# Attention with fp32 scores and transposes on row halves of the array, and the decay added by DVE

## The chip, the cores and the metric

The kernel runs on one core of one Trainium2 chip. Times are device microseconds. TensorE is PE, VectorE DVE, ScalarE ACT, GpSimd POOL; SP issues the DMAs. PEld is PE's loading of the stationary operand.

## The reference, cut to what matters

Three stages follow each other: causal attention with a decay, a dense mixture of eight experts, and a feed-forward stage. Only the first is touched. All is fp32.

```
B, H, S, D = 2, 8, 576, 64
scores = q @ k.T / sqrt(D)                  # per batch and head
cum    = cumsum(log(clip(f, 1e-4, 1)))      # per batch and head, over S
scores = scores + cum[i] - cum[j], masked to j <= i
attn   = softmax(scores);  x = attn @ v     # x: 1152 x 512
```

The term cum[i] is the same for a whole row, so the softmax doesn't change if it is left out.

## The kernel before

Work goes by query tiles: five per batch, ten in all (tile 0 to 9), of 128 queries (64 in tiles 4 and 5). A tile of queries that ends at position e sees the keys up to e, rounded up to whole blocks of 128: 128, 256, 384, 512 and 576 keys, in each batch. Within a tile the four pairs of heads are the units. A loop (line 588) makes two steps per unit, one for each head, and is a pipeline written out by hand: a step issues the exponential of the step before, the scores of its own head, a piece of filler, and in every second step the product with v of the unit three earlier (attend) and the transposes of the unit two earlier. Each engine runs its instructions in the order in which the loop issues them.

Products of queries and keys are made in fp32r, in which one pass of the array takes an operand of reduced precision. So q and k are split into a high and a low part (split, lines 308 to 319: a cast, and a subtraction on DVE or POOL), both are transposed on PE together (trans, lines 321 to 350, eight transposes of 128 columns per tile for q and eight for k), and the four tiles that two products need are evacuated or copied by DMA: scores (line 361) multiplies [q high; q high] with [k high; k low] (line 374) and [q low; constants] with [k high; rows of cum] (line 375). Two constants of -1 against two rows with cum in parts add the decay within the product. DVE then adds the mask, negates and takes the smallest value in one instruction (line 387); for 576 keys the scores lie in two PSUM tiles of 288 columns and DVE takes two. ACT makes the exponential and its sum (line 397), POOL multiplies with the reciprocal (normalize, line 413), PE transposes the weights p block by block of 128 keys (lines 429 and 440, in plain fp32), evac (line 273) moves them to SBUF on whichever of ACT and DVE a cost table thinks freer, and attend (line 453) multiplies them with v, the two heads of a unit on the two column halves of the array.

PSUM has eight banks: one for x, two for scores (ps_s), three for transposes (ps_t), two for the filler (ps_f). The filler (line 489) is the first expert on chunks 0 and 1 of x, 28 pieces of three products per chunk, one per step; it starts after tile 2 and after tile 6. Its weights are loaded and split during tiles 1 to 4 (wsplit, line 565). Warming products of the identity stand in front and in the first 16 steps (line 356).

All DMAs are issued by SP in program order: q and k of the tile after next (line 557), v, the rows of cum, the copies of halves (line 301), and the first experts' weights into the two tiles of the pool stage (line 54).

Of the kernel before, what the change touches and what calls it, by code (L numbers as in the profile page):

```python
# [83 lines left out]
def attention_moe_kernel(  # L84
# [46 lines left out]
    with ExitStack() as actx:  # L131
        ap1 = actx.enter_context(tc.tile_pool(name="ap1", bufs=1))
        rawp = actx.enter_context(tc.tile_pool(name="rawp", bufs=3))
# [28 lines left out]
        chl = pt0[1][:16, :, :S]  # L162
        zer = ap1.tile([16, 1], F32, name="zer")
        mask = ap1.tile([128, 704], F32, name="mask")


        sums4 = [ap1.tile([128, 3, 4], F32, name=f"sums{i}") for i in range(4)]
        cd = drp.tile([2, 16, S], F32, name="cd")


        KW = 832
        kbase = (256, 0)
        kt = kp.tile([128, H, KW], FR, name="kt")
        kbf = kp.tile([128, H, KW], FR, name="kb")
        kb = kbf[:96]
        qa = [kp.tile([128, 4, 128], FR, name=f"qa{i}") for i in range(3)]
        qb = [kp.tile([96, 4, 128], FR, name=f"qb{i}") for i in range(3)]

        def q_rows(i, engine=None):
            engine = engine or nc.gpsimd  # L180
            engine.memset(f(qb[i][64:96]), 0.0)
            engine.memset(f(qb[i][64:68]), -1.0)

        def k_rows(lo, hi, engine=None):
            (engine or nc.gpsimd).memset(f(kb[64:96, :, lo:hi]), 1.0)
# [17 lines left out]
        k_rows(256, 384, nc.vector)  # L203
        q_rows(0, nc.gpsimd)
        q_rows(1, nc.gpsimd)
        nc.vector.tensor_scalar(out=ft, in0=ft, scalar1=1e-4, scalar2=1.0, op0=ALU.max, op1=ALU.min)
        nc.vector.tensor_copy(out=idr, in_=idn)

        def cumulate(lo, hi, part=None):
            w = hi - lo  # L210
            if part != 1:
                cumulate_a(lo, hi, w)
            if part != 0:
                cumulate_b(lo, hi)

        def cumulate_a(lo, hi, w):
# [6 lines left out]
        def cumulate_b(lo, hi):  # L223
# [76 lines left out]
        def duplicate(o, i):  # L300
            nc.sync.dma_start(out=f(o), in_=f(i))

        def prep(kind, b, i, slots):
# [17 lines left out]
            def trans(g, early=False):  # L321
# [10 lines left out]
                if kind == "q":  # L332
                    a_, b_ = qa[slots[g]], qb[slots[g]]
                    if early and g:
                        cum_q(b, i, g, slots[g])
# [1036 lines left out]
```

## Time and profile before

| | |
|---|---|
| median of 3 runs | 1121.14 us (1119.29 to 1121.34) |
| profiled execution, first to last instruction | 1123.8 us |
| PE busy | 1109.8 us, 99% |
| DVE, ACT, POOL busy | 852.3, 504.3, 76.7 us |
| bytes moved by DMA | 98.93 MB |

The profiled execution has no other time than its span; it is one execution, and stands 2.7 us above the median of the runs. Products on PE are pipelined and their recorded durations overlap, so the distance between starts tells what one costs. An fp32 product (scores and x, not transposes) leaves two records each.

### The profile page before, as it was taken

Reading aid. Unit: us, or ns where it says so; the run is one execution under the profiler, and the core shown is the slowest. Engines: PE = TensorE matmul, PEld = TensorE weight load, DVE = VectorE, ACT = ScalarE, POOL = GpSimd, SP = SyncE. Lnnn points to the kernel's source line nnn. Section 1 sums busy time; section 2 is a strip of 40 time slices with the busy share of each in tenths; the row PEclk is TensorE's granted clock in tenths of the full one; section 3 lists DMA queues with packets and bytes.
Section 4 is the critical chain, followed back from the end, with each engine's and each line's share of the span. In section 5 each row is a group of like instructions: output and inputs, shape, how many; then the busy total and the mean of one; then the engine's idle time right before and its main releaser. Section 6 shows DMA issues by size and latency. Waiting matters only on the chain.

```text
span 1123.8 us, 17611 instructions
## 1 busy us (share of the span) xinstructions
PE 1109.8 (99%) x6608; PEld 981.3 (87%) x6608; DVE 852.3 (76%) x1850; ACT 504.3 (45%) x1128; POOL 76.7 (7%) x126
## 2 busy tenths in 40 slices
PE   8999999999999999999999999999999999999998
PEld 7677778989889898898988989899898988899996
DVE  7865655957786877868678686887868658998886
ACT  6766643245344253442534424243342335555554
POOL 5535420000000000000000000000000000000000
PEclk8899999999999999999999999999999999999999
DMA  5524212021332313323133241223311675000000
GB/s 124 145 65 105 53 39 76 20 75 42 128 110 77 124 50 130 105 75 132 49 113 110 86 140 58 94 96 111 122 67 57 205 253 198 1 29 1 29 1 29
DMA packets 78058, 98.93 MB, mean 88 GB/s; under 512 B 35190, under 2 KB 39046, under 8 KB 77974
## 3 DMA queue, kind: packets, MB, share of 16 engines
q1 hardware_dynamic: 77974, 97.81, 27.2%
q8 instruction: 52, 0.85, 0.3%
q14 instruction: 32, 0.26, 0.1%
HBM read 74.38 MB, written 19.21 MB: 83 GB/s over the span
## 4 chain that ended last, share of the span: by engine, by line
PE 93%; DVE 4%; ACT 1%; issue 1%; POOL 0%; DVEq 0%; ACTq 0%; POOLq 0%
PE pa L725 41%; PE pb L1080 28%; PE ph L695 11%; PE x L453 2%; PE pt L429 2%; PE pa L525 1%; PE sp L374 1%; PE ph L506 1%; PE pt L325 1%; DVE p L387 1%; PE sp L375 1%; PE x L862 0%; DVE r L973 0%; DVE r L967 0%; PE wt L359 0%
## 5 line engine op out<-in xcount | busy, mean ns | idle before, releaser
L725 PE MATMUL pa<-w2h,big 128*128 128x512 f32 x924 | 299.7, 393 | 1.2 <-DVE hid_b L703 1.2
L725 PEld LDWEIGHTS pa<-w2h,big 128*128 128x128 f32 x924 | 173.7, 188 | 39.7 <-DVE hid_b L703 1.5
L725 PE MATMUL pa<-w2l,big 128*128 128x512 f32 x528 | 207.2, 392 | 0.0
L1109 ACT COPY snap<-pb 128x288 f32<-128x288 f32 x168 | 66.4, 395 | 142.2 <-PE pb L1080 141.9
L725 PEld LDWEIGHTS pa<-w2l,big 128*128 128x128 f32 x528 | 99.3, 188 | 20.7
L703 DVE SCALAR_TENSOR_TENSOR big<-c,big 128x288 fp32r<-128x288 f32 x140 | 64.2, 459 | 69.4 <-ACT big L702 65.4
L702 ACT ACTIVATE big<-c 128x288 fp32r<-128x288 f32 x168 | 74.8, 445 | 91.8 <-DVE c L1114 89.0
L845 DVE SCALAR_TENSOR_TENSOR acc<-pa,P,acc 128x512 f32<-128x512 f32 x132 | 92.8, 746 | 27.2 <-PE pa L725 27.1
L1080 PE MATMUL pb<-xh,ss 128*128 128x288 f32 x448 | 103.9, 296 | 0.0
L1080 PE MATMUL pb<-tt,ss 128*128 128x288 f32 x672 | 103.7, 296 | 0.0
L1080 PEld LDWEIGHTS pb<-tt,ss 128*128 128x128 f32 x672 | 93.8, 188 | 1.0 <-ACT snap L1109 0.8
L1114 DVE TENSOR_TENSOR c<-pb,snap 128x288 f32<-128x288 f32 x168 | 75.9, 452 | 22.5 <-PE pb L1080 22.5
L824 ACT CAST db<-da 128x512 fp32r<-128x512 f32 x32 | 19.9, 621 | 147.8 <-DVE da L815 147.8
L1080 PEld LDWEIGHTS pb<-xh,ss 128*128 128x128 f32 x448 | 76.9, 188 | 0.6 <-DVE c L1114 0.3
L1080 PE MATMUL pb<-xl,ss 128*128 128x288 f32 x224 | 66.5, 297 | 0.0
L1080 PE MATMUL pb<-xh,w1l 128*128 128x288 f32 x224 | 66.2, 296 | 0.0
L1080 PE MATMUL pb<-xl,w1h 128*128 128x288 f32 x224 | 66.2, 295 | 0.0
L1080 PE MATMUL pb<-xh,w1h 128*128 128x288 f32 x224 | 66.1, 295 | 0.0
L725 PE MATMUL pa<-w2h,hid_b 128*128 128x512 f32 x150 | 58.6, 391 | 0.0
L397 ACT ACTIVATE p<-p,nmax 128x256 f32<-128x256 f32 (+6 forms) x80 | 48.4, 605 | 11.0 <-DVE nmax L387 8.4
L75 DVE TENSOR_TENSOR w2l<-stg,w2h 128x512 fp32r<-128x512 f32 x60 | 41.2, 690 | 15.9 <-ACT w2h L74 15.9
L413 POOL TENSOR_SCALAR p<-p,rs 128x256 f32<-128x256 f32 (+6 forms) x80 | 46.7, 596 | 66.4 <-DVE rs L409 42.2
(229 smaller groups left out, 2402.3 us busy)
## 6 DMA issues: line engine op xcount, KB each, us to landing
stg<-in_moe_w_dram SPq DMA_DIRECT2D x64, 512.0 KB
raw<-in_moe_w_in_dram SPq DMA_DIRECT2D x16, 512.0 KB
raw<-in_moe_w_out_dram SPq DMA_DIRECT2D x16, 512.0 KB
w_in_h<-db SPq DMA_DIRECT2D x16, 256.0 KB
w_in_l<-da SPq DMA_DIRECT2D x16, 256.0 KB
w_out_h<-db SPq DMA_DIRECT2D x16, 256.0 KB
w_out_l<-da SPq DMA_DIRECT2D x16, 256.0 KB
out_dram<-acc SPq DMA_DIRECT2D x9, 256.0 KB
```

The costliest lines, as they stand in the source:

```text
L75: (lo_engine or nc.vector).tensor_tensor(out=lo, in0=raw, in1=f(hi), op=ALU.subtract)
L397: nc.scalar.activation(out=p[:n, a, :nk], in_=p[:n, a, :nk], func=AF.Exp, bias=prev, scale=-1.0, accum_out=u["ssum"][:n, 0, a:a + 1],)
L413: nc.gpsimd.tensor_scalar(out=p[:n, a, :nk], in0=p[:n, a, :nk], scalar1=r[:n, a:a + 1], scalar2=1.0, op0=ALU.mult, op1=ALU.mult,)
L429: nc.tensor.transpose(out=pt[:, o + j * n:o + (j + 1) * n], in_=p[:n, a, j * 128:(j + 1) * 128], identity=idn[:n, :n],)
L695: nc.tensor.matmul(out=ph, lhsT=w[wn][kk][:, fs], rhs=x[c][:, kk], start=(kk == 0 and n == 0), stop=(kk == KD - 1 and n == 2),)
L702: nc.scalar.activation(out=hh, in_=ph, func=AF.Relu)
L703: nc.vector.scalar_tensor_tensor(out=hl, in0=ph, scalar=0.0, in1=f(hh), op0=ALU.max, op1=ALU.subtract)
L725: nc.tensor.matmul(out=pa, lhsT=a_[:, ts_], rhs=w[wn][ft_], start=(first and n == 0), stop=(last and n == 2),)
L845: nc.vector.scalar_tensor_tensor(out=acc[t], in0=pa, scalar=P[:, t, e:e + 1], in1=acc[t], op0=ALU.mult, op1=ALU.add)
L1080: nc.tensor.matmul(out=by_chunk(out_) if len(v_.shape) == 3 else out_, lhsT=u, rhs=v_, start=first and m == 0, stop=m == 5, skip_group_che ...
L1109: nc.scalar.copy(out=t, in_=bank["x", g])
L1114: nc.vector.tensor_tensor(out=t, in0=bank[of, g], in1=snap[with_, g], op=ALU.add)
```

## The change

q and k are no longer split. A row half of the array is its 64 rows 0 to 63 or 64 to 127. The function turn transposes two heads at a time in fp32: the first 64 queries (or keys) on one row half, the other 64 on the other, each into its own PSUM bank; one evacuation per q and per k follows. The heads of a unit then lie on partitions 0 to 63 and 64 to 127 of qt and kt, and scores multiplies both in one step, each on its row half, in fp32 into its own bank; for 576 keys the columns from the tile's start on go to a tile of ps_t. The transposes of p are cut the same way by query halves.

The decay goes out of the products. The negated cum is written to DRAM and read back by DMA to all 128 partitions: bias for the keys in front of the tile, diag for the tile's own keys, which POOL masks (mask_diag). DVE adds bias to the one part of a head's scores and diag to the other (largest), so each head but those of the first tile of a batch takes two instructions. For tile 0, where the DRAM copy would come late, diag is made by eight products of a selecting matrix (pick8) with cum and a DVE addition (spread).

The loop keeps its two steps per unit. Scores stand in the first; attend stands in every fourth step and takes two units; the filler is issued at the end of a step and no longer between scores and attend. ps_t has two tiles of two banks, ps_f one bank. Four of the filler's hidden tiles in its second chunk lie in tiles of stage, which are free when that chunk is done. The DMA copies of halves, the rows of cum and POOL's memsets for the constants are gone.

```
-        hlp = actx.enter_context(tc.tile_pool(name="hlp", bufs=2))
+        rawp = actx.enter_context(tc.tile_pool(name="rawp", bufs=4))
         kp = actx.enter_context(tc.tile_pool(name="kp", bufs=1))
+        mdp = actx.enter_context(tc.tile_pool(name="mdp", bufs=2))
         vp = actx.enter_context(tc.tile_pool(name="vp", bufs=6))
         pp = actx.enter_context(tc.tile_pool(name="pp", bufs=3))
-        ptp = actx.enter_context(tc.tile_pool(name="ptp", bufs=2))
+        ptp = actx.enter_context(tc.tile_pool(name="ptp", bufs=3))
         ps_x = actx.enter_context(tc.tile_pool(name="ps_x", bufs=1, space=PSUM))
         ps_s = actx.enter_context(tc.tile_pool(name="ps_s", bufs=2, space=PSUM))
-        ps_t = actx.enter_context(tc.tile_pool(name="ps_t", bufs=3, space=PSUM))
-        ps_f = actx.enter_context(tc.tile_pool(name="ps_f", bufs=2, space=PSUM))
+        ps_t = actx.enter_context(tc.tile_pool(name="ps_t", bufs=2, space=PSUM))
+        ps_f = actx.enter_context(tc.tile_pool(name="ps_f", bufs=1, space=PSUM))
...
+        KW = 704
+        kbase = (128, 0)
+        kt = kp.tile([128, 4, KW], F32, name="kt")
+        bias = kp.tile([128, H, KW], F32, name="bias")
+        hs1 = kp.tile([128, 12, 128], FR, name="hs1")
+        qt = [kp.tile([128, 4, 128], F32, name=f"qt{i}") for i in range(3)]
...
+        def negate(lo, hi):
+            nc.scalar.mul(out=neg[:, lo:hi], in_=cum[:, lo:hi], mul=-1.0)
+            nc.sync.dma_start(out=cd[:, lo:hi], in_=neg[:, lo:hi])
+        def load_bias(b, lo, hi):
+            nc.sync.dma_start(
+                out=bias[:, :, kbase[b] + lo:kbase[b] + hi],
+                in_=cd[b * H:(b + 1) * H, lo:hi].partition_broadcast(128),
             )
+        diag = {}
+        def span(b, i):
+            s0, n = QT[b][i]
+            return s0, min(S, -(-(s0 + n) // 128) * 128) - s0
+        def load_diag(ti):
+            b, i = tiles[ti]
+            s0, w = span(b, i)
+            diag[ti] = mdp.tile([128, H, 192], F32, tag="md", name="md")
+            nc.sync.dma_start(
+                out=diag[ti][:, :, :w], in_=cd[b * H:(b + 1) * H, s0:s0 + w].partition_broadcast(128)
+            )
+        def mask_diag(ti):
+            b, i = tiles[ti]
+            s0, w = span(b, i)
+            nc.gpsimd.affine_select(
+                out=diag[ti][:, :, :w], in_=diag[ti][:, :, :w], compare_op=ALU.is_ge, fill=NEG, base=0,
+                pattern=[[0, H], [-1, w]], channel_multiplier=1,
+            )
...
+        def turn(kind, ti, us=slice(0, 4)):
+            b, i = tiles[ti]
             s0, n = QT[b][i] if kind == "q" else KTL[i]
...
+            halves = n // 64
+            for u in range(us.start, us.stop):
+                for z in range(halves):
+                    zs = slice(64 * z, 64 * z + 64)
                     nc.tensor.transpose(
+                        out=pt[:, z, 64 * u:64 * u + 64], in_=raw[zs, 2 * u:2 * u + 2].rearrange("p h d -> p (h d)"),
+                        identity=idn[zs, zs],
                     )
+            cols = (us.stop - us.start) * n
+            src = pt[:, :halves, 64 * us.start:64 * us.stop].rearrange("p z (u t) -> p u z t", t=64)
+            if kind == "q":
+                evac(qt[ti % 3][:, us, :n].rearrange("p u (z t) -> p u z t", t=64), src, cols, 0.125)
+            else:
+                o = kbase[b] + s0
+                evac(kt[:, us, o:o + n].rearrange("p u (z t) -> p u z t", t=64), src, cols)
...
+        def scores(u):
+            b, h, n, nk, s0 = u["b"], u["h"], u["n"], u["nk"], u["s0"]
+            k0, g = kbase[b], u["h"] // 2
+            lhs = [qt[u["ti"] % 3][64 * a:64 * a + 64, g, :n] for a in range(2)]
+            sp = [ps_s.tile([128, 512], F32, tag="s", name="sp") for _ in range(2)]
+            rest = nk - s0 if nk > 512 else 0
+            if rest:
+                far2 = ps_t.tile([128, 2, 512], F32, tag="pt", name="far")
+                far = [far2[:, a] for a in range(2)]
+            def product(o, a, lo, hi):
+                nc.tensor.matmul(
+                    out=o, lhsT=lhs[a], rhs=kt[64 * a:64 * a + 64, g, k0 + lo:k0 + hi], start=True, stop=True
+                )
+            for a in range(2):
+                product(sp[a][:n, :nk - rest], a, 0, nk - rest)
+            if rest:
+                for a in range(2):
+                    product(far[a][:n, :rest], a, s0, nk)
+            u["p"] = pp.tile([128, 2, S], F32, tag="p", name="p")
+            u["ssum"] = sums4[(4 * u["ti"] + h // 2) % 4]
+            u["parts"] = []
+            for a in range(2):
+                parts = [(sp[a][:n, :s0], bias[:n, h + a, k0:k0 + s0], 0, s0)] if s0 else []
+                d = far[a][:n, :rest] if rest else sp[a][:n, s0:nk]
+                parts.append((d, diag[u["ti"]][:n, h + a, :nk - s0], s0, nk))
+                u["parts"].append(parts)
+        def largest(u, a):
+            n, p = u["n"], u["p"]
             prev = 3.0e38
+            spent("dve", 110 + 67 + 1.05 * u["nk"])
+            for s_, t_, lo, hi in u["parts"][a]:
                 am = small.tile([128, 1], F32, tag="nmax", name="nmax")
                 nc.vector.tensor_tensor_reduce(
+                    out=p[:n, a, lo:hi], in0=s_, in1=t_, scale=-1.0, scalar=prev, op0=ALU.add, op1=ALU.min,
+                    accum_out=am[:n],
                 )
                 prev = am[:n]
...
+            nb = (nk + 127) // 128
+            halves = n // 64
+            whole = [(a, j) for a in range(2) for j in range(min(nb, 4))]
+            pt = ps_t.tile([128, 2, 512], F32, tag="pt", name="pt")
+            def block(o, z, a, j):
+                zs, w = slice(64 * z, 64 * z + 64), KTL[j][1]
+                nc.tensor.transpose(out=o[:w], in_=p[zs, a, j * 128:j * 128 + w], identity=idn[zs, zs])
+            for o, (a, j) in enumerate(whole):
+                for z in range(halves):
+                    block(pt[:, z, 64 * o:64 * o + 64], z, a, j)
+            jw = min(nb, 4)
+            src = pt[:, :halves, :128 * jw].rearrange("p z (a m) -> p a z m", a=2)
+            dst = pT[:, :, :jw * n].rearrange("p a (j z t) -> p a z j t", z=halves, t=64)
+            parts = [(dst, src)] if 2 * jw * n <= 512 else [(dst[:, a], src[:, a]) for a in range(2)]
...
+                hs = [tuple(hs1[:, 6 * i + 3 * j:6 * i + 3 * j + 3] for j in range(2)) for i in range(2)]
             for i in range(4):
+                if len(hs) == i:
+                    t = stage.tile([128, 2, 512], FR, tag="stg", name="spare")
+                    hs.append(tuple(t[:, j, :CH].rearrange("p (j t) -> p j t", j=3) for j in range(2)))
...
+        def spread(h0):
+            pb = ps_s.tile([128, 512], F32, tag="s", name="pb")
+            for h in range(4):
+                nc.tensor.matmul(
+                    out=pb[:, 128 * h:128 * h + 128], lhsT=pick8[:, h0 + h], rhs=cum[:, :128],
+                    start=True, stop=True,
+                )
+            nc.vector.tensor_tensor(
+                out=diag[0][:, h0:h0 + 4, :128], in0=pb.rearrange("p (h t) -> p h t", h=4),
+                in1=mask.unsqueeze(1).to_broadcast([128, 4, 128]), op=ALU.add,
+            )
+        def turn_half(g):
+            for kind in "qk":
+                turn(kind, 0, slice(2 * g, 2 * g + 2))
+        diag[0] = mdp.tile([128, H, 192], F32, tag="md", name="md")
+        cumulate(128, S)
         warm(8)
+        turn_half(0)
+        spread(0)
         load_v(0, 0)
+        negate(0, S)
+        load_diag(1)
+        load_bias(0, 0, 128)
+        first = [lambda: spread(4), lambda: turn_half(1)]
...
+        for s in range(2 * nu + 10):
...
+                if not a:
+                    scores(units[pi])
+                largest(units[pi], a)
             if s < 16:
                 warm(1)
+            if not a and pi % 2 == 0 and 4 <= pi < nu + 4:
+                for w in units[pi - 4:pi - 2]:
+                    attend(w)
+                if w["h"] == H - 2:
+                    x_out(w)
...
+                    next_loads(ti + 2)
                 elif (st, a) == (0, 1):
+                    turn("q", ti + 1)
                 elif (st, a) == (1, 1):
+                    turn("k", ti + 1)
                     load_v(nb_, ni)
+                if (st, a) == (0, 1) and ti:
+                    load_diag(ti + 1)
+                    lo = [0, 0, 64, 192, 320][ni] if nb_ else 128 * max(ni - 1, 0)
+                    hi = [0, 64, 192, 320, 448][ni] if nb_ else 128 * ni
+                    if hi > lo:
+                        load_bias(nb_, lo, hi)
+                elif (st, a) == (3, 0):
+                    mask_diag(ti + 1)
+            fill()
```

## Rows read from the trace of the kernel before

**Rows 1.** The head of the page: the span, and busy time of each engine.

```profile
span 1123.8 us, 17611 instructions
PE 1109.8 (99%) x6608; PEld 981.3 (87%) x6608; DVE 852.3 (76%) x1850; ACT 504.3 (45%) x1128; POOL 76.7 (7%) x126
```

**Rows 2.** Busy us by stretch: length, PE, PEld, DVE, ACT, POOL, granted clock, DMA.

```profile
9.50:21.80 12.30, 10.22 (x64) 9.22 (x64) 8.37 (x32) 9.64 (x28) 4.53 (x12) 0.72 0.76 161
21.80:42.00 20.20, 19.72 (x170) 15.67 (x170) 17.04 (x61) 16.89 (x48) 12.60 (x23) 1.00 0.72 174
42.00:64.80 22.80, 21.72 (x129) 15.76 (x128) 14.72 (x39) 12.57 (x33) 9.36 (x12) 0.70 0.34 88
64.80:161.20 96.40, 94.70 (x811) 75.21 (x809) 64.36 (x234) 63.97 (x163) 41.88 (x58) 1.00 0.30 70
161.20:178.00 16.80, 16.80 (x134) 12.60 (x132) 4.42 (x9) 4.80 (x10) 1.47 (x2) 1.00 0.11 32
```

**Rows 3.** The same view around the fall of PE's granted clock (PEclk).

```profile
20.80:41.30 20.50, 20.02 (x173) 15.77 (x171) 16.90 (x61) 17.22 (x50) 13.47 (x24) 1.00 0.72 175
41.30:48.10 6.80, 5.72 (x50) 4.08 (x48) 6.03 (x19) 5.38 (x15) 4.19 (x6) 1.00 0.36 80
48.10:61.80 13.70, 13.70 (x62) 10.08 (x60) 8.81 (x23) 7.55 (x19) 4.53 (x7) 0.50 0.29 70
```

**Rows 4.** Order of time on PE: start us, us, line, operation, records.

```profile
139.05 0.40 PE L374 MATMUL sp<-kt,qa 128*128 128x512 f32 x1
...
139.53 0.34 PE L506 MATMUL ph<-xh,big 128*128 128x384 f32 x1
...
139.87 0.34 PE L506 MATMUL ph<-xh,big 128*128 128x384 f32 x1
140.14 1.09 PE L453 MATMUL x<-pT,v 128*64 128x128 f32 x16
141.16 1.09 PE L429 MATMUL pt<-idn,p 128*128 128x128 f32 x8
142.01 0.38 PE L374 MATMUL sp<-kt,qa 128*128 128x288 f32 x1
```

**Rows 5.** Order of time on PE, a tile of 64 queries.

```profile
83.84 0.71 PE L429 MATMUL pt<-idn,p 64*128 64x64 f32 x8
84.39 0.27 PE L440 MATMUL pt<-idn,p 64*64 64x64 f32 x2
```

**Rows 6.** Order of time on PE, transposes of a split q.

```profile
88.52 0.46 PE L325 MATMUL pt<-idr,hl 128*128 128x128 f32 x4
88.81 0.24 PE L374 MATMUL sp<-kt,qa 128*64 128x128 f32 x1
```

**Rows 7.** Order of time on DVE, the first reduction of scores.

```profile
11.04 0.27 DVE L387 CUSTOM_DVE_ANT_0 p<-sp,mask 128x128 f32<-128x128 f32 x1
```

**Rows 8.** Groups of instructions by shape to 178 us: count, busy us, mean ns.

```profile
L276 ACT ACTIVATE qa<-pt 64x512 fp32r<-64x512 f32 x12 | 7.0, 586 | 5.7 <-PE pt L325 4.9 <-DVE qb L280 0.8
L288 DVE CAST hl<-raw 128x512 fp32r<-128x512 f32 x8 | 3.7, 469 | 0.0
```

**Rows 9.** The same view, DVE's reductions of scores.

```profile
L387 DVE CUSTOM_DVE_ANT_0 p<-sp,mask 128x512 f32<-128x512 f32 x16 | 10.9, 685 | 7.0 <-PE sp L375 6.9
L387 DVE CUSTOM_DVE_ANT_0 p<-sp,mask 128x384 f32<-128x384 f32 x16 | 8.7, 547 | 0.1
L387 DVE CUSTOM_DVE_ANT_0 p<-sp,mask 128x128 f32<-128x128 f32 x8 | 2.2, 280 | 0.5 <-PE sp L375 0.5
L387 DVE DVE_READ_ACCUMULATOR2_ANT nmax<- 128x1 f32 x72 | 5.9, 82 | 0.0
```

**Rows 10.** DMA queue to 180 us: packets, MB, share of 16 engines.

```profile
q1 hardware_dynamic: 38134, 15.22, 35.8%
```

**Rows 11.** Groups by shape, the mask made on POOL.

```profile
L242 POOL TENSOR_SCALAR_AFFINE_SELECT mask<-mask 128x704 f32<-128x704 f32 x1 | 0.8, 774 | 0.1
```

**Rows 12.** Waits by releaser, 9.5 to 178 us: total, times, longest us.

```profile
PEld sp L374 <- DVE nmax L387: 5.6, 15, 1.0
```

More of the change, by code (lines that the diff above doesn't have):

```diff
@@ L236, in attention_moe_kernel @@
-        cumulate(0, 128)
-        early = stage.tile([128, 2, H, D], F32, tag="stg", name="early")
-        for a, (nm, src) in enumerate((("q", q), ("k", k))):
-            nc.sync.dma_start(out=early[:, a], in_=src[0, :, 128:256, :].rearrange("h p d -> p h d"))
-            raws[nm, 0, 128] = early[:, a]
-        nc.gpsimd.memset(mask, 0.0)
-        nc.gpsimd.affine_select(
-            out=mask, in_=mask, compare_op=ALU.is_ge, fill=NEG, base=512,
-            pattern=[[-1, 704]], channel_multiplier=1,
-        )
@@ L249, in attention_moe_kernel @@
+        cumulate(0, 128)
+        load_raw("q", q, 0, 128, 128)
+        load_raw("k", k, 0, 128, 128)
         for t in sums4:
             nc.gpsimd.memset(t, 1.0)
[L251 to L252 removed]
+        nc.gpsimd.memset(ones, 1.0)
         busy["pool"] = 10000.0
[L255 to L258 removed]
@@ L410, in normalize @@
             spent("dve", 350)
-            busy["pool"] += 2 * (90 + 1.1 * nk)
             for a in range(2):
@@ L420, in transposes @@
             pT = ptp.tile([128, 2, 5 * 128], F32, tag="pT", name="pT")
-            nb = min(nk // 128, 4)
-            w = nb * n
-            both = 2 * w <= 512
-            for a in range(2):
-                if a == 0 or not both:
-                    pt = ps_t.tile([128, 512], F32, tag="pt", name="pt")
-                o = a * w if both else 0
-                for j in range(nb):
-                    nc.tensor.transpose(
-                        out=pt[:, o + j * n:o + (j + 1) * n], in_=p[:n, a, j * 128:(j + 1) * 128],
-                        identity=idn[:n, :n],
-                    )
-                if not both:
-                    evac(pT[:, a, :w], pt[:, :w], w)
@@ new lines, in transposes @@
+            for o, (a, j) in enumerate(whole):
[5 more added lines that the diff above has]
+            parts = [(dst, src)] if 2 * jw * n <= 512 else [(dst[:, a], src[:, a]) for a in range(2)]
+            for d_, s_ in parts:
+                if len(d_.shape) == 5:
+                    s_ = s_.rearrange("p a z (j t) -> p a z j t", t=64)
+                else:
+                    s_ = s_.rearrange("p z (j t) -> p z j t", t=64)
+                evac(d_, s_, 2 * jw * n // len(parts))
@@ L437, in transposes @@
             if nk > 512:
-                p5 = ps_t.tile([128, 2, 256], F32, tag="pt", name="pt")
+                if halves > 1:
+                    pt = ps_t.tile([128, 2, 512], F32, tag="pt", name="pt")
                 for a in range(2):
-                    nc.tensor.transpose(out=p5[:64, a, :n], in_=p[:n, a, 512:576], identity=idn[:n, :n])
-                evac(pT[:64, :, 4 * n:5 * n], p5[:64, :, :n], 2 * n)
+                    for z in range(halves):
+                        zo = z if halves > 1 else 1
+                        block(pt[:, zo, 64 * a:64 * a + 64], z, a, 4)
@@ L476, in gate @@
                 )
[L477 removed]
+            lg = ap1.tile([2 * E, CH], F32, tag="lg", name="lg")
             nc.vector.tensor_copy(out=lg, in_=g[:16, :CH])
@@ L587, in attention_moe_kernel @@
         nu = len(units)
-        for s in range(2 * nu + 8):
+        for s in range(2 * nu + 10):
             pi, a = divmod(s, 2)
```

235 lines of the change are left out of this document (40 added, 195 removed).

## The prediction

> **What bounds the kernel now.** I read the head of the page first, then the busy time by stretch, then the order of time on the single engines. The page shows TensorE (PE) busy for 1109.8 of 1123.8 us [rows 1]. The change touches attention only. Cut where the first score product of a query tile starts, the table by stretch [rows 2] gives: tile 0 12.3 us, tiles 1 and 2 20.2, tile 3 22.8, tiles 4 to 9 96.4, the tail 16.8; the 945.8 us behind 178.0 keep their instructions. So the first 178.0 us are what can move. They have three limits. In tiles 0 to 2 no engine is full by itself: DVE and ACT are busy for 17.0 and 16.9 of the 20.2 us of tiles 1 and 2, and PE's busy figure counts pipeline latency. In tile 3 PE's granted clock fell: 1.00 up to 41.3 us, 1.00 still in the 6.8 us in which PE had only 5.7 us of busy time, then 0.50 from 48.1 to 61.8 us [rows 3]; 0.50 is the 1.2 GHz level. From tile 4 on PE has work without pause (94.7 of 96.4 us), since pieces of the first expert fill it.
>
> **PE's prices.** One step at full clock [rows 4]: the two fp32r products of a head, 512 columns each, take from 139.05 to 139.53, so 0.24 us each and 0.96 for a pair of heads. Sixteen records of x from 140.14 to 141.16 take 1.02 us, 64 ns each; eight transposes from 141.16 to 142.01 take 106 ns each. Both stream 128 fp32 columns, so a record of x costs 0.6 of a transpose: the two heads of x lie on column halves of the array, and these work side by side. A transpose of 64 rows alone takes 69 ns (eight from 83.84 to 84.39) [rows 5]. The transposes of q and k are four in 0.29 us at best [rows 6].
>
> Transposes of the weights p: 24 blocks of 128 rows per head, 192 in all, become 384 half transposes. If the halves work side by side, as column halves do, a pair costs about 69 ns: 192 x 37 ns = 7 us less. If they don't, 138 ns: 6 us more. Those of q and k fall from 160 of 73 ns or more to 80 places (64 pairs, 16 singles) of 69: 11.7 - 5.5 = 6 us less, or with no overlap 2 us less.
>
> Scores: an fp32 product has two records (as x has), each 106 ns per 128 columns, so 512 columns cost 2 x 424 = 848 ns. Two heads on row halves side by side take 0.85 us instead of 0.96; one after the other 1.70. The keys of the ten tiles are 29 blocks of 128, each met by four pairs of heads: 116 x 0.24 = 28 us now, 116 x 0.212 = 25 with overlap (3 less), 49 without (21 more).
>
> Against these stands the change of array shape. The last filler product before x starts at 139.87 and x at 140.14: 0.27 us, where the two before it took 0.17 each [rows 4], and the first pair of x is slow again, so I put a change at 0.15 us. Now a pair of heads costs two (into x and out). With the change, steps run scores (row halves), x (every second pair of heads), filler (whole array), transposes (row halves), filler: 4.5. The filler runs in 28 of 40 pairs of heads: 28 x 2.5 x 0.15 = 10 us more. Whether going between row halves and the whole array costs as much as column halves do, no row shows; its bounds are 0 and 10 us, and I take 7.
>
> The Trainium skill says it does: "TensorEngine Tiling (Array Packing)", Key Properties, has a change of tiling mode drain the engine, while using another tile of the same mode does not. The trace agrees for the column halves (0.27 against 0.17 us). By that rule the term is 10 us and the sum 3 us worse.
>
> **The sum by stretch.** Start and tile 0: splitting, two evacuations for q, the halves' copies and the fp32r constants go. The first reduction now ends no earlier than 11.3 us [rows 7]. The first transposes need only the loads; the new decay tile wants eight fp32 records and one DVE addition. I put that reduction about 2.5 us earlier, and tile 0, whose second half of the heads waits for casts and four evacuations, about 2.5 shorter: -5 (bounds -8 and 0).
>
> Tiles 1 and 2: per tile two casts (0.46 on DVE) and four of six evacuations of q and k at 0.59 go [rows 8], about 3.6 us of ACT and DVE; the reduction of each head in two parts (128 columns 0.28, 384 columns 0.55 us, each with its 0.08 read) costs 0.22 more than the one of 512 in 0.69 [rows 9], so +1.8 per tile. Net 1.8 per tile over two engines, -2 for both tiles. But each tile now waits for two broadcasts of decay, 128 partitions x 8 heads of 512 B, 1024 packets and 512 KB. A packet of this stage takes 0.358 x 16 x 180 us / 38134 = 27 ns [rows 10] at 399 B; so 1024 x 27/16 = 1.7, by bytes 2.2 us, each. Issued in step 1 of a tile behind q and k and wanted by POOL's mask in step 6 and by DVE at the next tile's start, they are late in the short tiles by 0 to 2 us, and POOL's queue holds the normalization behind the mask (704 columns took 0.77 us, so 1024 some 1.1 [rows 11]). Likeliest -1 (bounds -3 and +5).
>
> Tile 3: 22.8 us, of which 13.7 lie at half clock. PE has less to stream there, so the clock will fall as well, probably earlier. At half clock a pair of heads of 512 keys wants 2 x (0.85 + 0.8 + 0.55) = 4.4 us and switching, some 18.5 for the tile: -4 (bounds -7 and +3).
>
> Tiles 4 to 9, PE's queue: transposes of p about -5 (those of 64 rows stay), of q and k -3.5, scores -2; of the 5.6 us in which scores wait for DVE [rows 12], mostly where 576 keys need four products in two buffers, -3; changes of shape +7. The product accumulators of the filler have one bank instead of two: at each of 14 group ends the next three products wait for ACT's and DVE's 1.1 us unless scores or transposes cover it: +1 (0 to +8). Sum -5.5 (bounds -17 and +8).
>
> Tail and hand-over: transposes -1; x waits one step more, +1; and the filler now holds both stage tiles until the attention ends, so the next expert's first weights are loaded then instead of at 139 us: +1.5 (0 to +4).
>
> -5 - 1 - 4 - 5.5 + 1.5 = -14, of which I take 1 off for waits that I can't place: -13. The profiled span would go from 1123.8 to 1110.8 us. That execution lies 2.7 us above the median of the runs, 1121.14; the difference applied to the median gives 1108.
>
> **Rivals.** (a) Row halves do not overlap. For it: no row shows row halves. Against: column halves do, and every pair of halves writes two banks. From tile 3 on PE decides: 92 of the 116 score blocks, +20 us, and the transposes, 69 ns for each of some 190 pairs, +13: 33 us on the forecast, 1141 us, slower. It decides as soon as a pair of halves takes over 100 ns. Chance 0.10.
>
> The Trainium skill speaks against this rival: "TensorE: Matmul & The Clock Gate", Part 3, has row-packed products start some 4 ns apart and four of them reach 3.07 times the rate. The trace shows it for column halves alone (64 against 106 ns).
>
> (b) The clock stays down. Lighter PE work in tiles 1 and 2 drops it before 41 us, and again between the two fillers in tile 7. 13.7 us at half clock are 6.9 us lost where PE is full; 20 us more of it leave -3: 1118 us. For it: the clock fell behind PE's lightest stretch, 5.7 of 6.8 us busy [rows 3]. Against: the warming products stay in tiles 0 and 1. Chance 0.14.
>
> (c) The broadcasts are slow: 128 partitions read the same 4 KB. At three times the packet time each takes 5 to 6.6 us, two per tile; then tiles 1 to 3 wait 5 us each and tiles 4 to 9 one each: +20 on the forecast, 1128 us, slower. Chance 0.07.
>
> (d) The single filler bank and the two double-bank transpose tiles (in tiles of 576 keys one of them holds scores) stop PE's queue 0.15 us in each of 84 steps: the gain is spent, 1121 us. Chance 0.07.
>
> **How the numbers follow.** The forecast has 0.62, with 1100 to 1116 as its own range. A measurement of this kernel tells 0.2% (2.2 us) from no change. Faster by more than that: 0.62 and most of (b), 0.73. Within it: most of (d) and some of (b), 0.09. Slower: (a), (c) and a little of (d), 0.18. The range takes in (b) and (d) and the low bounds of tiles 4 to 9: 1097 to 1124 us.
>
> **What would show it.** Right: half transposes start in pairs, about 65 to 70 ns per pair; a pair of scores of 512 keys takes about 0.9 us; the first reduction ends before 9.5 us; the work after attention starts some 13 us before 178.0. Wrong: halves that follow each other at 60 ns or more; POOL or DVE waiting for the decay's DMA at tile starts; a granted clock of 0.50 longer than 13.7 us after tile 0; filler products waiting for their bank. An attention stage as long as now makes the prediction wrong.

## The result, and the profile after

The change made the kernel slower: 1134.01 us, median of four executions (1128.33 to 1139.62), against 1121.24; the ratio is 1.0115 with a 95% interval of 1.0074 to 1.0156. The forecast was 1108 us. The traced execution is the fastest of the four, and that of [rows 1] a slow one of its kernel (see below), so the spans lie only 2.8 us apart:

```profile
span 1126.6 us, 17823 instructions
PE 1104.4 (98%) x6776; PEld 956.1 (85%) x6776; DVE 837.8 (74%) x1903; ACT 488.8 (43%) x1096; POOL 59.3 (5%) x107
```

The table by stretch of the kernel after, with the columns of [rows 2], is cut at the first scores of tiles 0, 1, 3 and 4 and at the end of attention:

```profile
6.40:18.80 12.40, 11.70 (x73) 9.26 (x74) 4.78 (x25) 4.75 (x19) 2.91 (x7) 0.57 0.86 187
18.80:41.50 22.70, 19.93 (x195) 12.81 (x194) 15.10 (x81) 14.36 (x43) 8.91 (x19) 0.94 0.95 215
41.50:63.75 22.25, 19.98 (x159) 11.81 (x156) 13.33 (x52) 12.13 (x31) 6.21 (x10) 0.85 0.23 66
63.75:181.15 117.40, 109.31 (x1067) 72.65 (x1067) 65.12 (x280) 61.87 (x159) 37.51 (x57) 1.00 0.32 78
```

The first scores stand 3.1 us earlier, at 6.4 us. That is all that was gained. Tile 0 takes as long as before (12.4 us), tiles 1 and 2 take 2.5 us more, tile 3 0.5 less, and the stretch from tile 4 to the end 117.4 us, where the last two lines of [rows 2] add up to 113.2. There DVE, ACT and POOL are each busy for less time than before and PE's busy time is shorter by 2 us; PE stands idle for 8.1 us where it was idle for 1.7. Behind attention nothing changed: 945.4 us against 945.8.

PE's order of time shows that the array itself does what was forecast (one unit of tile 8, to be held against [rows 4]; start us, us, line, records):

```profile
129.48 1.13 PE L319 MATMUL sp<-kt,qt 64*128 64x512 f32 x4
130.54 1.53 PE L419 MATMUL x<-pT,v 128*64 128x128 f32 x24
132.00 0.44 PE L474 MATMUL ph<-xh,big 128*128 128x384 f32 x1
132.28 0.33 PE L474 MATMUL ph<-xl,big 128*128 128x384 f32 x1
132.45 0.34 PE L474 MATMUL ph<-xh,big 128*128 128x384 f32 x1
132.72 0.59 PE L383 MATMUL pt<-idn,p 64*128 64x64 f32 x12
133.14 0.42 PE L289 MATMUL pt<-idn,raw 64*128 64x64 f32 x8
```

Twelve half transposes take 0.42 us, 70 ns per pair: the halves work side by side. Four records of scores take 1.06 us from start to start, 0.2 more than the 0.85 that the prediction worked out for them, and the last filler product ahead of the half transposes takes 0.27 us where the one ahead of it took 0.17. So a change of shape costs 0.1 to 0.2 us; it was put at 0.15.

PE's waits by releaser, here in tiles 4 and 5 (63.7 to 100 us; total, times, longest us), show what is new; the kernel before had one line in these tiles (64.8 to 97.4 us), shown behind them:

```profile
PE pt L383 <- ACT pT L266: 2.5, 3, 1.0
PE pt L289 <- ACT pT L266: 1.8, 1, 1.8
PE pt L383 <- DVE pT L270: 0.8, 1, 0.8
```

```profile
PE sp L374 <- DVE nmax L387: 0.4, 2, 0.2
```

In the order of time of PE, and of ACT, one such wait of a unit with 64 queries and 576 keys:

```profile
83.56 0.71 PE L383 MATMUL pt<-idn,p 64*128 64x64 f32 x8
85.29 0.24 PE L383 MATMUL pt<-idn,p 64*64 64x64 f32 x1 [1.02 <-ACT pT L266]
```

```profile
83.90 0.78 ACT L353 ACTIVATE p<-p,nmax 64x576 f32<-64x576 f32 x1 [0.49 <-DVE nmax L343]
84.58 0.19 ACT L353 ACTIVATION_READ_ACCUMULATOR p<-p,nmax 64x1 f32 x1
84.67 0.56 ACT L266 COPY pT<-pt 128x512 f32<-128x512 f32 x1
```

The eight whole blocks are done by 84.3; the two transposes of the last block go into the other bank of the same tile and wait until ACT, busy with an exponential, has copied the first bank. In [rows 5] the last block followed the eight at once, in a tile of its own.

The second line, 1.8 us once in tile 4, is turn: both double-bank tiles of ps_t are still held when it wants one. In tile 9 (128 queries, 576 keys) the last block meets the same, twice (waits of PE from 6 to 181 us, then the order of time of PE and of DVE):

```profile
PE pt L383 <- DVE nmax L343: 1.8, 2, 1.1
```

```profile
163.35 0.71 PE L383 MATMUL pt<-idn,p 64*128 64x64 f32 x16
164.84 0.30 PE L383 MATMUL pt<-idn,p 64*64 64x64 f32 x4 [0.77 <-DVE nmax L343]
```

```profile
164.70 0.08 DVE L343 DVE_READ_ACCUMULATOR2_ANT nmax<- 128x1 f32 x1
```

There the last block takes a new tile of two banks, and the other one holds scores of a later unit (far) until DVE has reduced them. The two double-bank tiles thus cost 3.6 us of waits.

DVE's reductions, by shape up to 181 us (count, busy us, mean ns), against [rows 9]:

```profile
L343 DVE DVE_READ_ACCUMULATOR2_ANT nmax<- 128x1 f32 x120 | 10.0, 83 | 0.0
L343 DVE CUSTOM_DVE_ANT_0 p<-sp,md,nmax 128x128 f32<-128x128 f32 x24 | 8.4, 351 | 1.2
L343 DVE CUSTOM_DVE_ANT_0 p<-sp,bias 128x256 f32<-128x256 f32 x8 | 3.3, 412 | 0.6 <-PE sp L319 0.5
```

A second part of 128 columns takes 351 ns, not the 280 of a first part; it takes its starting value from the first part's result (nmax), and whether that is the reason was not tested. With 83 ns for its read, 384 keys cost 0.93 us of busy time (412 + 83 + 351 + 83) where one instruction and its read cost 0.63. So a second part adds 0.30 us to a head; I had put 0.22.

### The profile page after: what moved, and what is told of

The parts are those of the page before. It is cut to its first block, busy times and chain, and to the rows that moved or that the text cites. A ratio compares the mean times of both kernels' runs of the same rounds, so it can differ in the third digit from the quotient of the medians.

```text
span 1126.6 us, 17823 instructions
## 1 busy us (share of the span) xinstructions
PE 1104.4 (98%) x6776; PEld 956.1 (85%) x6776; DVE 837.8 (74%) x1903; ACT 488.8 (43%) x1096; POOL 59.3 (5%) x107
## 4 chain that ended last, share of the span: by engine, by line
PE 94%; DVE 4%; ACT 1%; issue 1%; POOL 0%; DVEq 0%; ACTq 0%; POOLq 0%
PE pa L693 41%; PE pb L1048 28%; PE ph L663 11%; PE sp L319 3%; PE x L419 3%; PE ph L474 2%; PE pa L493 2%; PE pt L383 1%; DVE p L343 1%; PE wt L306 1%; PE pt L289 0%; ACT p L353 0%; PE x L830 0%; DVE r L941 0%; DVE xl L428 0%
## 5 line engine op out<-in xcount | busy, mean ns | idle before, releaser
L1082 DVE TENSOR_TENSOR c<-pb,snap 128x288 f32<-128x288 f32 x168 | 75.9, 452 | 22.5 <-PE pb L1048 22.5
L75 DVE TENSOR_TENSOR w2l<-stg,w2h 128x512 fp32r<-128x512 f32 x60 | 41.2, 689 | 15.9 <-ACT w2h L74 15.9
L319 PE MATMUL sp<-kt,qt 64*128 64x256 f32 (+6 forms) x160 | 46.1, 527 | 4.7 <-DVE nmax L343 4.3
```

Of the source, the lines that this page charges most:

```text
L75: (lo_engine or nc.vector).tensor_tensor(out=lo, in0=raw, in1=f(hi), op=ALU.subtract)
L319: nc.tensor.matmul(out=o, lhsT=lhs[a], rhs=kt[64 * a:64 * a + 64, g, k0 + lo:k0 + hi], start=True, stop=True)
L1082: nc.vector.tensor_tensor(out=t, in0=bank[of, g], in1=snap[with_, g], op=ALU.add)
```

## Experiments

Theory 1 is PE's granted clock, theory 2 PE's own order (waits and changes of shape), theory 3 the decay's broadcasts. Times are medians; "from tile 4 on" is the stretch from tile 4's first scores to the end of attention.

**The changed kernel again** (e0, no edit).

> The changed kernel itself, six more executions beside the others of this study. Theory 1 (the granted clock): its time goes with the mean clock that each execution shows. An execution at a mean of 0.99 or more is near 1128 us, one at 0.98 near 1137 us, so the time rises some 6 us per 0.01 of clock (half clock over 22 us costs 11 us where TensorE is full), and the median follows from how long the clock was down in tiles 0 to 5. Theory 2 (TensorE's queue waits for its own order: changes of array shape, transposes that wait for a PSUM tile, scores that wait for reductions in two parts): the times stay 1128 us or more even where the clock is 0.997, and the clock explains the rest of the spread only. Theory 3 (the decay broadcasts come late): the spread goes with the landing of the broadcasts and not with the clock.

Measured: 1131.16 us, ratio 1.0104 (1.0067 to 1.0141). Its seven executions, with their mean clock: 1126.4 (0.994), 1128.1 (0.991), 1130.0 and 1131.2 (0.997), 1137.0 (0.982), 1140.3 twice (0.978). The three long ones had the lowest clock, so theory 1 holds for them; but at 0.994 and 0.997 the time is still 5 to 10 us above before, so there is something else. What can make 0.997 slower than 0.994 is told in the last section.

**The last block's transposes ahead of the evacuation** (e1).

```
+            if nk > 512 and halves == 1:
+                for a in range(2):
+                    block(pt[:, 1, 64 * a:64 * a + 64], 0, a, 4)
             jw = min(nb, 4)
```

> In units of 64 rows and 576 keys the two transposes of the last block are issued before the evacuation of the first four blocks and no longer behind it. Theory 2: eight units (tiles 4 and 5) lose a wait of 0.9 to 1.1 us each in TensorE's order, half of them uncovered: 4 to 5 us less than the changed kernel of the same call, and the stretch from the first score of tile 4 to that of tile 6 falls from 38.4 to about 34 us. Theories 1 and 3: no more than 1 us, since the wait would be taken by the clock or by the broadcasts instead.

Measured: 1126.71 us (1.0049; 1.0031 to 1.0067), 4.5 less than the changed kernel, and no execution above 1131.2. The expectation counted eight units; there are four, in tile 4 alone. In PE's order of time all ten transposes now follow each other:

```profile
87.45 0.82 PE L383 MATMUL pt<-idn,p 64*128 64x64 f32 x10
88.20 0.44 PE L476 MATMUL ph<-xh,big 128*128 128x384 f32 x1
```

The stretch from tile 4 on, all at full clock, in the changed kernel (the traced execution of the run above) and in this one:

```profile
61.80:179.24 117.44, 109.37 (x1068) 72.67 (x1067) 65.13 (x280) 62.00 (x159) 37.69 (x57) 1.00 0.33 78
```

```profile
67.63:182.13 114.50, 109.53 (x1067) 72.42 (x1067) 65.31 (x280) 61.48 (x159) 37.69 (x57) 1.00 0.33 80
```

2.9 us of the 4.5 are this wait; tiles 4 and 5 fell from 38.4 to 35.4 us, where about 34 was expected. The other 1.6 I put down to the clock, since the executions of 1137 to 1140 us are gone; this is not shown.

**Filler in one place per unit** (e2).

```
-            fill()
             if a:
                 continue
             ...
+            fill(2)
```

> The filler products come six at a time behind the scores of every pair of heads, not three behind the scores and three behind the transposes: one or two changes of array shape less in each of 28 pairs of heads. Theory 2 with a change at 0.15 us: 28 x 1.5 x 0.15 = 6 us less than the changed kernel of the same call (between 4 and 8). If a change of shape costs nothing that TensorE's waits do not hide, or if the filler covered waits between transposes and scores: no difference, or up to 4 us slower. Theories 1 and 3: within 1 us, the clock as before.

Measured: 1142.25 us (1.019; 1.0166 to 1.0214), 11 us slower: a miss. The filler between transposes and scores covers DVE's reductions, and this is worth more than the changes of shape it costs. Without it the second head's scores wait for a bank; in PE's order of time:

```profile
122.04 0.46 PE L383 MATMUL pt<-idn,p 64*128 64x64 f32 x8
122.34 0.86 PE L319 MATMUL sp<-kt,qt 64*128 64x384 f32 x2
123.84 0.88 PE L319 MATMUL sp<-kt,qt 64*128 64x384 f32 x2 [0.64 <-DVE nmax L343]
```

At full clock this is little: tiles 6 and 7 take 0.3 and 1.0 us more than in the trace of e0. Most of the loss lies in tiles 4, 5 and 8 (1.8, 5.6 and 3.8 us), in each of which the clock lay at 0.50 for a while (in tile 5 from 90.0 to 107.1 us). How much of that is the waits themselves was not separated.

**More warming products.** First `if s < 28: warm(1)` in the changed kernel (e3), then, on top of e1, `warm(20)` at the start and `if s < 28: warm(2)` (x8).

> The warming product of 128 columns is issued in steps 0 to 27 (until the filler starts) and no longer in steps 0 to 15 alone. Theory 1: TensorE's clock stays up in tiles 2 and 3; where the profile showed 20 us at half clock up to 49 us there are under 8, the spread of the executions shrinks to some 3 us and the median falls by 5 to 8 us. Theory 2: twelve products more, each with two changes of shape, are in the way: 12 x 0.5 = up to 6 us slower, at best no difference. Theory 3: no difference.

> On top of e1, the start has 20 warming products instead of 8, and steps 0 to 27 have two each instead of one in steps 0 to 15. Theory 1: the clock stays up through tiles 0 to 3 (mean clock 0.995 or more in every execution), the spread shrinks to 3 us and the median falls to 1122 or 1123 us. Theory 2: the clock may rise, but the products and their changes of shape are in the way: 1127 to 1131 us. Theory 3: no difference.

Measured: e3 1128.48 us (1.0093; 1.0056 to 1.0129), with executions from 1125.6 to 1128.9 and three at 1141; x8 1129.58 (1.0084; 1.0061 to 1.0108), all but one between 1129.2 and 1129.8 at a clock of 0.996 or 0.997. Theory 1 had both gain 4 us or more with a spread of 3 us. The steadier clock came in x8 alone and the gain in neither: the products stand in PE's queue and cost at least what they give (x8's first scores start at 9.1 us, e1's at 6.5).

**No broadcasts after tile 0** (x5), on top of e1; bias is treated like diag, and both are filled once. This kernel leaves out the decay and the mask of tiles 1 to 9.

```
-            diag[ti] = mdp.tile([128, H, 192], F32, tag="md", name="md")
-            nc.sync.dma_start(
-                out=diag[ti][:, :, :w], in_=cd[b * H:(b + 1) * H, s0:s0 + w].partition_broadcast(128)
-            )
+            diag[ti] = diag[0]
```

> On top of e1 (transposes of the last block ahead of the evacuation), the fifteen broadcasts of the decay after tile 0 are left out: the two decay tiles are filled once, so the decay and the mask of tiles 1 to 9 are not computed; the mask instruction of POOL and both parts of every reduction stay. Against e1's median of 1126.7 us. Theory 3 (broadcasts late): tiles 1 and 2 fall from 11 us to under 10 each and the time by 4 us or more, to 1122 or less, with a smaller spread. Theories 1 and 2: at most 1.5 us less, since DVE waits for few landings and TensorE's order stays.

Measured: 1128.36 us (1.0071; 1.0046 to 1.0097), no less than e1. In its trace tiles 1, 2 and 3 take 12.9, 12.3 and 23.5 us and the stretch from tile 4 on 114.5; in e1's they take 12.9, 12.3, 23.6 and 114.5. Theory 3 falls: broadcasts that took 6 to 7 us from issue to landing (e0) were in time.

**One reduction per head**, on top of e1, against zeros (x6); this kernel leaves out the decay and the mask wherever a head with 512 keys or fewer had two parts.

```
+                if s0 and not rest:
+                    parts = [(sp[a][:n, :nk], zero[:n, :nk], 0, nk)]
```

> On top of e1, every reduction of a head with 512 keys or fewer is one instruction over all keys against a tile of zeros, not two (decay and mask are left out there; the broadcasts still run). Theory 2: each of some 56 heads gains 0.2 to 0.3 us of DVE, and in tiles 1 to 3, 6 to 8, where the scores of the next pair wait for both heads' reductions, TensorE waits less: 4 to 8 us less than e1 (1119 to 1123 us). Theory 1: within 1 us of e1 in the median, the spread as before. Theory 3: less by what x5 shows, since here too DVE no longer waits for the landings in those tiles.

Measured: 1121.77 us (1.0011; 0.9997 to 1.0025), 4.9 less than e1, as theory 2 had it. The same with the whole computation kept (x11): POOL writes the masked block into the row of bias itself (mask_diag with another output) and restores it later.

```
+                out=bias[:, hs, o:o + w], in_=diag[ti][:, hs, :w], compare_op=ALU.is_ge, fill=NEG, base=0,
...
+                nc.gpsimd.tensor_copy(out=bias[:, hs, o:o + n], in_=diag[ti][:, hs, :n])
...
+                dec = diag[0][:n, h + a] if not u["ti"] else bias[:n, h + a, k0:k0 + nk]
+                parts = [(sp[a][:n, :nk - rest], dec[:, :nk - rest], 0, nk - rest)]
```

> On top of e1, one reduction per head with the decay kept: POOL writes the masked block from the broadcast tile into the decay row itself, and later restores the unmasked block from the same tile, four heads at a time; one broadcast per tile and no longer two. If the second part of the reduction is what x6 removed: 1121 to 1123 us as x6 (1121.8). If POOL's extra copies (four instructions of 512 to 768 columns per tile, some 2.2 us) hold up the normalization in its queue: 1124 to 1127 us. Theory 3 would have it gain more than x6.

Measured: 1121.07 us (0.9996; 0.9982 to 1.0011). The two repairs together take 10 us off the changed kernel and make it level with before. From tile 4 on its trace has 1.6 us less than e1, and the waits for double-bank tiles, 1.8 us in tile 4 (turn) and 1.8 in tile 9, are still there (the stretch, then PE's waits in it):

```profile
61.35:174.24 112.89, 108.13 (x1068) 71.64 (x1068) 59.88 (x230) 61.55 (x160) 43.11 (x72) 1.00 0.27 64
```

```profile
PE pt L392 <- DVE nmax L352: 1.8, 2, 1.1
PE pt L297 <- ACT pT L274: 1.8, 1, 1.8
```

**Whole transposes of p**, on top of e1 (x9) and of x11 (x12), and x12 with `warm(2)` in steps 0 to 15 (x13).

```
+                nc.tensor.transpose(
+                    out=pt[:, 0 if both else a, o:o + n], in_=p[:n, a, j * 128:j * 128 + 128], identity=idn[:n, :n]
+                )
```

> On top of e1, the transposes of the weights are whole 128-row transposes again (one record each, as in the kernel before), all else of the change stays. It undoes one part. If the half transposes bring what their 69 ns per pair say (192 x 37 ns = 7 us, less one change of shape per pair of heads): 3 to 7 us slower than e1, 1130 to 1134 us. If going between row halves and the whole array costs as much as the overlap gives: within 1.5 us of e1.

> x11 together with whole 128-row transposes of the weights (x9): of the change only the scores, the transposes of q and k by row halves and the decay on DVE stay. Theory 2: the two gains add: x9 was 0.9 us under e1, x6 5 us under it, so about 1121 us. Theory 1: x9's executions lay within 2 us of each other, so the spread stays near 2 us and the median falls to 1119 or 1120 us, level with before.

> x12 with two warming products instead of one in each of steps 0 to 15. Theory 1: the clock rises earlier in tile 0 or stays up in tile 1, and the time falls by 2 to 4 us against x12, to under 1119 us, faster than before. Theory 2: sixteen products more of 0.11 us at full clock, in front of other work: 0 to 3 us slower than x12.

Measured: x9 1125.84 us (1.0049; 1.003 to 1.0067), executions from 1125.6 to 1127.4, so not the 3 to 7 us slower than e1 that the price of a pair would have; x12 1121.27 (0.9994; 0.9976 to 1.0012), as theory 2 had it; x13 1124.57 (1.0026; 1.0012 to 1.0039), a miss for theory 1. From tile 4 on the trace of x9 has 116.00 us, at full clock, 1.5 more than e1:

```profile
62.27:178.27 116.00, 111.97 (x948) 77.19 (x947) 65.41 (x280) 61.31 (x160) 37.49 (x57) 1.00 0.32 78
```

The half transposes gain 1.5 us there, which I had put at 5, and lose it again ahead of tile 4.

**The half transposes alone, in the kernel before**: in all tiles (x7), and from tile 3 on (x14: under `else` of `if u["ti"] < 3`).

```
+                pts = [ps_t.tile([128, 512], F32, tag="pt", name="pt") for _ in range(halves)]
+                for o in range(2 * nb):
+                    a, j = divmod(o, nb)
+                    for z in range(halves):
+                        zs = slice(64 * z, 64 * z + 64)
+                        nc.tensor.transpose(
+                            out=pts[z][:, 64 * o:64 * o + 64], in_=p[zs, a, j * 128:(j + 1) * 128],
+                            identity=idn[zs, zs],
+                        )
```

> The kernel before with one part of the change alone: the transposes of the weights go as pairs by row halves into two banks (two one-bank tiles, one per half), everything else as it was. If the pairs bring what they cost less (192 x 37 ns = 7 us) and a change of shape more per pair of heads takes back 40 x 0.15 = 6 us where TensorE is full: within 2 us of before. Theory 2: no gain, 0 to 3 us slower, since with half transposes the filler no longer follows in the same shape. Theory 1: slower by 3 us or more with a lower and more scattered clock, since half-array work is what lets the clock fall.

> The kernel before with the pairs by row halves for the transposes of the weights from tile 3 on, and whole transposes in tiles 0 to 2 (x7 had pairs in all tiles). Theory 1: x7 was 2.9 us slower because the clock lay at half from 14.1 to 34.6 us of its tiles 0 to 2, while its stretch from tile 4 on was 3.0 us shorter than before; with whole transposes ahead of tile 3 the clock is before's and the 3 us stay: 1118 us, faster than before. Theory 2: the half transposes cost as much in switching as they give: 1120 to 1122 us, and tiles 0 to 2 do not depend on them.

Measured: x7 1123.76 us (1.0019; 1.0006 to 1.0033); x14 1118.61 (0.9976; 0.9961 to 0.9991), 3.3 us below the kernel before, as theory 1 had it. The two traces, each with the stretch of low clock and the stretch from tile 4 on:

```profile
14.10:34.60 20.50, 19.64 (x114) 16.28 (x113) 11.63 (x49) 13.12 (x43) 9.69 (x23) 0.50 0.56 124
65.47:175.60 110.13, 108.02 (x1063) 83.74 (x1060) 68.24 (x246) 68.08 (x175) 43.78 (x60) 1.00 0.28 66
```

```profile
16.40:23.20 6.80, 6.80 (x37) 6.25 (x35) 3.74 (x19) 3.64 (x13) 4.64 (x11) 0.50 0.88 180
60.09:169.90 109.81, 107.99 (x1063) 83.73 (x1059) 68.16 (x246) 68.31 (x175) 43.74 (x60) 1.00 0.28 67
```

From tile 4 on both have 3.1 to 3.4 us less than the 113.2 of before. With half transposes in tiles 0 to 2 the clock lay at the 1.2 GHz level for 20.5 us and these tiles took 38.1 us; without, for 6.8 us, and 33.4. The mean clock of x7's executions is 0.986 to 0.994, of x14's 0.988 to 0.998. So half transposes in the light tiles 0 to 2 cost clock, and from tile 3 on, where the filler keeps PE busy, they pay. Whether the clock falls because half of the array is in use or because PE is busy for less time was not separated.

**Whole transposes in tiles 0 to 2** of x11 (x15) and of the changed kernel (x16); the edit is x9's under `if u["ti"] < 3`.

> x11 (the change with both repairs: last block first, one reduction per head) with whole transposes of the weights in tiles 0 to 2 and pairs from tile 3 on. Theory 1: tiles 0 to 2 as in x12, the stretch from tile 4 on as in x11 (1.4 us shorter than x12's): 1119 to 1120 us, with a spread of 3 us. Theory 2: between x11 and x12, 1121 us.

> The changed kernel with one edit alone: whole transposes of the weights in tiles 0 to 2. Theory 1: the executions at 1137 to 1140 us (mean clock 0.978 to 0.982) vanish, since they come from the lighter start; all lie from 1125 to 1130 us. Theory 2: the same scatter from 1126 to 1140 us, median 1131 us, since nothing in the waits from tile 3 on has changed.

Measured: x15 1120.95 us (0.9992; 0.998 to 1.0004), no better than x11, as theory 2 had it. In its trace the clock lies at 0.50 from 67.7 to 71.1 us, right behind turn's wait in tile 4, and this tile takes 22.5 us instead of the 21.0 of x11. x16 1128.28 (1.0063; 1.0039 to 1.0087), four executions from 1125.6 to 1128.4 and two at 1134.7. Theory 1 had the long ones vanish: half right. The times of 1137 to 1140 us are gone, and the traced execution, one of the two long ones, shows where the rest comes from:

```profile
70.00:85.70 15.70, 12.22 (x122) 8.59 (x122) 10.15 (x37) 9.25 (x22) 5.44 (x7) 1.00 0.22 50
85.70:106.20 20.50, 18.98 (x144) 13.55 (x142) 4.83 (x24) 6.32 (x21) 4.21 (x7) 0.50 0.36 88
```

Behind the stretch of tile 4 in which PE waits (12.2 of 15.7 us busy) the clock falls for 20.5 us, and from tile 5's first scores to tile 6's it is 23.6 us instead of the 15.9 of the trace after:

```profile
86.25:102.10 15.85, 14.34 (x161) 9.94 (x161) 5.46 (x30) 7.49 (x24) 5.13 (x10) 1.00 0.50 117
```

So tile 4's waits can cost twice: 2.9 us themselves (those that e1 removes), and in this execution 7.7 us of clock behind them. The traces of the changed kernel have the same waits and keep their clock there, so the fall does not always follow; that its executions of 1137 to 1140 us come from it is likely, not shown.

## Why the prediction was wrong

**The forecast by stretch**, against the two traces: start and tile 0 -5, measured -3.0; tiles 1 and 2 -1, measured +2.5; tile 3 -4, measured -0.5; from tile 4 to the end of attention -4, measured +4.2.

**The array's prices were right.** Pairs of halves at 70 ns (put at 69), scores of a pair at 0.85 us and 0.2 for the change of shape, the start 3 us earlier (put at 2.5). Rival (a) is refuted. The page "TensorE: Matmul & The Clock Gate" of the Trainium skill, Part 3, had row-packed products side by side: the trace agrees (70 ns per pair, 69 ns for one alone).

**The failed step is "waits -3" in tiles 4 to 9.** I took the 5.6 us in which scores wait for DVE [rows 12] as the waits there are, and gave the change 3 of them back. That line did fall, from tile 4 to the end of attention from 4.1 us to 0.2 (before, then after):

```profile
PEld sp L374 <- DVE nmax L387: 4.1, 12, 0.5
```

```profile
PEld sp L319 <- DVE nmax L343: 0.2, 1, 0.2
```

But the change brought losses of its own: the last block behind the evacuation, 2.9 us (e1), and the second part of the reductions, 1.6 us from tile 4 on (x11 against e1; PE's idle time shows only 0.2 of it, 5.0 us against 4.8). That is +4.5 in place of -3, and the 3.6 us of waits for double-bank tiles come on top, within the rest below. I had priced the second part in tiles 1 and 2 alone, and not read the order in which transposes() issues the last block against its evacuation. The Trainium skill, "TensorEngine Tiling (Array Packing)", Performance Considerations, warns that tiling speeds the array but not the evacuation of PSUM. The 1.02 us here are a wait for an evacuation too, but its place in the order made it and not its speed: e1 keeps the same copy.

**"Transposes of p about -5" was too large.** With the tail's -1 they were put at -6. At full clock, from tile 4 on, they gave 3.1 to 3.4 us in the order of before and 1.5 in that of the change. All else there (q and k -3.5, scores -2, shapes +7, single bank +1, x and loads of the tail +2.5: +5) came to +1.2: the 112.9 of x11 and the 1.5 of the halves, against 113.2. This holds the 3.6 us of waits for double-bank tiles, which no run took out. So where -4 was forecast (-6 + 5 - 3), the stretch came out at +4.2 (-1.5 + 1.2 + 4.5).

**Tile 3's -4 was not there to be had in most executions.** The traced execution of before had 13.7 us of tile 3 at half clock [rows 3] and 20.5 in all. It stood some 4.4 us above the median, not 2.7: I had held its span against times, and in the 94 later executions of before the time is 1.7 to 1.9 us longer than the span. Of these 94, 75 have a mean clock of 0.995 or more and take 1119 to 1122 us; the 13 at 0.992 or less take 1122 to 1127. I priced the change against a slow one and moved the gain to the median. x14's trace, with tiles 0 to 2 as before and half transposes from there on, has tile 3 at full clock in 17.6 us, not 22.8.

**Tiles 0 to 2.** Tile 0 was to be 2.5 us shorter. In the trace after, whose clock lay at half from 8.1 to 21.7 us, it is no shorter; in that of e0, with 6.8 us at half, it is 1.6 shorter. Tiles 1 and 2, put at -1, take 1.6 us more even at full clock (21.8 us in e0's trace against 20.2).

**Rival (b), the clock, had the right mechanism and the wrong price.** I gave it 0.14 and 1118 us. In the changed kernel the clock falls in tiles 0 to 3 and, as x16 suggests, in some executions again in tile 5 behind tile 4's waits: 1126 to 1140 us for one program. Rival (c) is refuted by x5. Of rival (d) the single bank shows no wait of the filler; the double-bank tiles cost 3.6 us in three places (1.8 in tile 4, 1.1 and 0.8 in tile 9), not 0.15 in each of 84 steps. I had given it 0.07.

**The account in medians**: 1131.2 for the changed kernel; 4.5 off for the order of the last block, 5.6 off for the second parts, gives 1121.1, and before took 1120.8. So the whole loss is these two details with what they do to the clock, and what is left of the change is worth nothing in this order, which still holds the 3.6 us of waits for double-bank tiles. Of the 5.6 us, 1.6 lie from tile 4 on, and tile 2, at full clock in both traces, is 0.7 us shorter with one reduction per head (10.9 us in e0, 10.1 in x11); how much of the rest is DVE's time and how much clock was not separated.

## What to carry to other kernels

When an engine's queue is kept in order, price a change by what each of its new instructions waits for, not only by its duration: two transposes behind an evacuation and one 0.3 us instruction more per head undid a gain on the busiest engine. Where the clock of TensorE can fall, ask what the change does to the lightest stretch of the kernel, and check whether the traced execution is a typical one before counting a low clock as time to be gained. A part that shortens the full stretches and lightens the thin ones is best used in the full ones alone: here half transposes from tile 3 on gave 3.3 us, and everywhere cost 2.9.

## What the runs showed of the hardware

PE's clock at the start is not in the record of the granted clock until it first changes. In x6 the table shows a clock of 1.00 from 7.7 to 20.0 us, but the warming products tell otherwise (the stretch, then PE's order of time; two records per product of 128 columns):

```profile
7.70:20.00 12.30, 11.91 (x68) 9.38 (x68) 4.46 (x23) 4.32 (x17) 2.30 (x5) 1.00 0.92 187
```

```profile
14.93 1.22 PE L308 MATMUL wt<-idn 128*128 128x128 f32 x4
...
25.06 0.71 PE L308 MATMUL wt<-idn 128*128 128x128 f32 x4
```

Four records end 1.22 us after the first starts, later 0.71; a record starts 213 ns after the one ahead of it at first and 112 ns at the end, the 1.2 and the 2.4 GHz level. So this execution of x6 ran its tile 0 at half clock without a sign of it. Its mean clock of 0.997 is too high for that reason, and it took 1123.2 us where one with 0.994 took 1119.3. The changed kernel's 1131.2 us at 0.997 and 1126.4 at 0.994 fit this; the first was not traced. In the traces of x5 (at 19.33 us) and x16 (at 19.54 us) four warming records still take 1.22 us as well, so their mean clocks are too high too. The Trainium skill, "TensorE: Matmul & The Clock Gate", Part 1, calls the clock's records unreliable; x6 shows one way in which they are.
